# Stage 1's weight sums moved into the last first layer of stage 0, and the f64 conversion paced 11 and 17 steps a stage

## The chip, the cores and the metric

The kernel runs on one core of one Trainium2 chip. The metric is the time of one execution on the device in microseconds. The core has five instruction streams that work in parallel and wait for one another by semaphores: PE (matrix products), DVE (vector), ACT (activations and copies), POOL (elementwise), and SP, which here only issues DMAs. Each executes its own stream in order, so an instruction that waits holds all that stand behind it on its engine.

## The reference, cut to what matters

```
attention: scores = q k^T / 8, a window of 64 positions back, softmax, times v
x = attn_out as (1152 tokens, 512)
moe:   p = probs / sum(probs);  out = sum over e of p[:, e] * (relu(x @ w1[e]) @ w2[e])
       w1: (4, 512, 1024)   w2: (4, 1024, 512)
moe2:  h = out @ w_in;  g = max(h, 0) + alpha * min(h, 0);  result = g @ w_out
       w_in: (512, 2048)    w_out: (2048, 512)
```

All of it is wanted in float32. The weights of the last part come as float64 and are read as pairs of 32-bit words.

## The kernel before

**Stages.** The hidden dimension is cut into stages of 512 columns: stages 0 to 7 for the four experts, 8 to 11 for the last part. A stage has a first layer (x times w1) and a second layer (h times w2, added up in `acc`). Every float32 operand is split into a rounded high part and a low part (names ending in h and l); a product is three matmuls of the parts. The high part is made by ACT (`split`, L219), the low part by DVE (`low`, L212).

**Stage 0** runs with the attention, in four chunks of tokens: `LC(c)` is the first layer of chunk c (4 units), `BC(c)` its second layer (2 or 3 units). The last chunk, `LC(3)` and `BC(3)`, comes after the attention.

**Stages 1 to 11** make the first layer by seven half-size products of sums and differences of blocks in place of eight (units `A(s,p,i)`, i from 0 to 6, p=0 for tokens 0 to 511 and p=1 for 512 to 1151, each for two halves u of the columns). For that, sums of the weight blocks (`w_sums`, L187, tile `sr`, four instructions for each u) and of the token blocks (`x_sum`, L384, tile `tr`) are needed, and both are split: weights into `wf` by `w_split`, in the parts A11, A22 and SA1 (SA1 is the four sums), tokens into `xt`. The results of the products are combined in `product`: s, z and u are copies of the first, second and third product by ACT (L433) before the next product adds onto the same PSUM bank; later DVE adds the fourth, fifth and sixth to them (`total`, L437). So PE's third product (bank X again) waits for ACT's copy s, the fifth for ACT's copy u, and the seventh, in bank X once more, waits until DVE's total z has read the bank. The second layer has units `B(s,p,t)`, four for p=0, five for p=1, 12 matmuls each; DVE adds each to `acc` (L559).

**The order of the work** is written out by hand: `order` lists the units, `plan(unit, fn, ...)` hangs side work behind a unit, and every engine's stream is the order in which this Python code issues. From the last first layer on, the low part of a split is issued one unit after its high part (`late["wait"]`, `settle`). A weight load (`load_w`, tile `ws`, two buffers) is issued behind the last unit that uses the tile two loads earlier.

**The conversion.** The f64 weights of stages 8 to 11 are turned into float32 in 32 blocks during stages 1 to 7 (`conv_steps`) and stored in DRAM (`cv`). One block takes three steps, called a, b and c here:

- a: DVE L289 and POOL L290, L291 finish the block before; then ACT L277 and L278 begin this one from its loaded words (`wd`, two buffers).
- b: DVE L280 and L281, and SP's store of a finished block.
- c: DVE L284, and SP's load of the block two further on.

`pace` says how many steps follow a unit: one after each of the first three product units of A(s,0) and of A(s,1) from stage 2 on, two after each of the nine B units of stage 1, one after each B unit of stages 2 to 6. So stage 1 has 18 steps and stages 2 to 6 have 15 each, stage 7 has 6.

**Order around stage 1.** The sums of stage 1's weights hang on unit X1, between LC(3) and BC(3), on DVE for u=0 and on POOL for u=1. The token sums and splits for p=1 hang on the four units of LC(3) and the first three of A(1,0), all sums on POOL.

Of the kernel before, what the change touches and what calls it, by code (L numbers as in the profile page):

```python
# [26 lines left out]
def tile_kernel(ctx, tc, q, k, v, probs, w1, w2, w_in, w_out, alpha, out):  # L27
    nc = tc.nc
# [26 lines left out]
    NCH = len(CHUNK) - 1  # L55
# [33 lines left out]
    xr = [xr0, xr1[:, 0:KD * LEN[1]].rearrange("p (k t) -> p k t", k=KD)]  # L89
# [5 lines left out]
    for c in range(1, NCH):  # L95
        n = CHUNK[c + 1] - CHUNK[c]
# [68 lines left out]
    A11, A12, A22, SA1, SA2, SA3, SA4 = range(7)  # L165

    def w_block(s, u, i, j):
        t = ws_t[1, s]
        if s >= S1:
            return t[:, 2 * u + i, 2 * j * P:2 * (j + 1) * P].rearrange("p (k m) -> p k m", k=2)  # L170
        c = (2 * u + i) * P
        return t[:, 2 * j:2 * j + 2, c:c + P]

    def w_sums(s, u, e):
        if (s == 1 or s >= S1) and u == 1:
            t4 = late["mid"].tile([P, 1024], F32, tag="wd", bufs=2, name=f"sr{s}_{u}").rearrange(
                "p (o k m) -> p o k m", o=4, k=2)
# [389 lines left out]
    def raw2(p):  # L567
        return late[f"raw{p}"]
# [7 lines left out]
    with tc.manual_schedule():  # L576
# [104 lines left out]
        def plan(unit, fn, tid, *args):  # L681
            work.setdefault(at[unit], []).append((fn, tid, args))
# [2 lines left out]
            plan(("LC", 0, f), split_w2, (2, 0), 0, f)  # L685
        for s in range(1, NST):
            if s == 1:
                for u, e in enumerate((nc.vector, nc.gpsimd)):
                    plan(("X1",), w_sums, (1, s), s, u, e)
                b = [("BC", NCH - 1, t) for t in range(2)]  # L690
                for u, part, unit in ((0, A11, ("X1",)), (0, A22, ("X1",)), (0, SA1, b[0]), (1, A11, b[0]), (1, A22, b[0]), (1, SA1, b[1])):
                    plan(unit, w_split, (1, s), s, u, part)
            else:
                b = [("B", s - 1, x, t) for x in range(2) for t in range(NTT[x])]
                if s == S1 + 1:
                    b = [("B", S1, 1, t) for t in (3, 3, 4, 4, 0, 1)]
# [23 lines left out]
        for unit, p, splits, sums, (o, w) in changes:  # L720
# [5 lines left out]
            for f in sums:  # L726
                e = nc.vector if unit[0] == "B" and p else nc.gpsimd
                plan(unit, lambda *a: x_sum(a[0], raw2(a[0]), *a[1:]), (0, S1) if p == 0 else None, p, f, o, w, e)
        lc = [("LC", NCH - 1, f) for f in range(NF)] + [("A", 1, 0, i) for i in range(3)]
        for n, splits, sums in ((0, (0,), (1,)), (1, (0, 1), (2,)), (2, (2,), (3,)), (3, (), (4,)),  # L730
                                (4, (3,), ()), (5, (5,), ()), (6, (4,), ())):
            for o, w in half[1]:
                for f in splits:
                    if f == 0 and o == w * n:
                        plan(lc[n], x_first, None, 1, xr[1], o, w)
                    elif f:
                        plan(lc[n], x_split, None, 1, xr[1], f % 5, o, w)
# [25 lines left out]
        def pace(op, s=0, p=0, i=0):  # L763
            if op not in "AB" or s >= S1 or (s, op) in ((1, "A"), (S1 - 1, "B")):
                return 0
            return int(i < 3) if op == "A" else 1 + (s == 1)

        late["steps"] = conv_steps()
        pend = []
        for i, unit in enumerate(order):  # L770
            op = unit[0]
# [35 lines left out]
            for _ in range(pace(*unit)):  # L807
                next(late["steps"], None)
# [48 lines left out]
```

## Time and profile before

| what | value |
| --- | --- |
| median of 3 runs | 647.77 us (647.1 to 648.51) |
| the profiled execution | 647.18 us |
| its span, first to last instruction | 645.4 us |
| mean granted PE clock | 0.992 |
| busy: PE, DVE, ACT, POOL | 616.2, 469.8, 310.1, 288.9 us |

The profile is of one execution. Busy time counts instructions in flight; matmuls overlap, so the time that a run of them takes is read from the starts. The granted clock is a share of PE's full speed. In the timeline "[4.32 <-ACT s L433]" behind a row means that the engine had been idle 4.32 us and that the instruction it then waited for was ACT's on line 433. Where several matmuls stand in one row, xcount tells how many.

### The profile page before, as it was taken

The page shows a single profiled execution, that of the slowest core. Times are in us where ns is not written, and L with a number is a line of the kernel's source. Part 1 is how long each engine was busy: PE and PEld are TensorE (multiplying, and loading weights), DVE is VectorE, ACT ScalarE, POOL GpSimd, SP SyncE. Part 2 cuts the span into 40 slices and gives each one's busy share as a digit, 9 for nine tenths or more (in the row PEclk, how much of TensorE's full clock was granted, in tenths as well). Part 3 has the DMA queues.
Part 4 walks back from the last instruction along what each step waited for, and adds up shares of the span by engine and source line. Part 5 has one row for each costly group of instructions (what it writes and reads, how often), then busy time and mean ns, then how long its engine had stood idle before and what let it go on. Part 6 is the DMA issues. An engine that isn't in the chain of part 4 may idle for free.

```text
span 645.4 us, 10914 instructions
## 1 busy us (share of the span) xinstructions
PE 616.2 (95%) x4032; PEld 549.8 (85%) x4032; DVE 469.8 (73%) x937; ACT 310.1 (48%) x783; POOL 288.9 (45%) x303
## 2 busy tenths in 40 slices
PE   4799998997899999999999999999999999999998
PEld 3678887986898988988988988988897998988986
DVE  4765648879889889889889888866685474574652
ACT  5545534542561651641742642634766670760730
POOL 4645663235455345335435435524744290390440
PEclk9899999999899999999999999999999999999999
DMA  9841002215533433434334234001301011010012
GB/s 327 287 149 60 16 2 100 97 49 177 166 114 102 161 125 116 136 132 135 121 120 160 102 115 163 34 1 66 132 0 66 2 67 65 1 66 1 2 49 99
DMA packets 31654, 62.61 MB, mean 97 GB/s; under 512 B 2288, under 2 KB 11760, under 8 KB 30576
## 3 DMA queue, kind: packets, MB, share of 16 engines
q1 hardware_dynamic: 31600, 61.90, 27.6%
q8 instruction: 32, 0.52, 0.3%
q14 instruction: 22, 0.18, 0.1%
HBM read 51.14 MB, written 10.75 MB: 96 GB/s over the span
## 4 chain that ended last, share of the span: by engine, by line
PE 73%; DVE 16%; ACT 4%; DMA 3%; issue 2%; POOL 1%; SPq 0%; DVEq 0%; ACTq 0%; POOLq 0%
PE o L540 39%; PE X L426 17%; PE Z L426 7%; PE W L426 4%; DVE w2l L212 3%; DMA ws<-in_moe_w_dram 2%; PE oc L528 2%; PE h L495 2%; DVE ct L280 2%; DVE wfl L212 2%; DVE ct L284 2%; DVE ct L281 2%; ACT p L321 1%; ACT w2h L219 1%; POOL hl L521 1%
## 5 line engine op out<-in xcount | busy, mean ns | idle before, releaser
L540 PE MATMUL o<-w2h,hl 128*128 128x512 f32 (+1 forms) x400 | 155.7, 389 | 0.6 <-POOL hl L521 0.5
L540 PE MATMUL o<-w2l,hh 128*128 128x512 f32 (+1 forms) x400 | 155.6, 389 | 0.4 <-ACT hh L520 0.4
L540 PE MATMUL o<-w2h,hh 128*128 128x512 f32 (+1 forms) x400 | 154.9, 387 | 0.0
L290 POOL TENSOR_TENSOR ct<-ct 128x512 f32<-128x512 f32 x32 | 41.5, 1296 | 147.4 <-DVE ct L289 66.0
L540 PEld LDWEIGHTS o<-w2h,hl 128*128 128x128 f32 x400 | 75.1, 188 | 18.4 <-POOL hl L521 3.2
L540 PEld LDWEIGHTS o<-w2l,hh 128*128 128x128 f32 x400 | 75.1, 188 | 15.1 <-ACT hh L520 0.6
L540 PEld LDWEIGHTS o<-w2h,hh 128*128 128x128 f32 x400 | 75.2, 188 | 14.7
L559 DVE SCALAR_TENSOR_TENSOR acc<-o,pn,acc 128x512 f32<-128x512 f32 x63 | 47.1, 748 | 31.8 <-PE o L540 31.5
L426 PE MATMUL X<-xth,wfl 128*128 128x256 f32 (+1 forms) x264 | 58.7, 304 | 6.9 <-ACT s L433 4.3
L212 DVE SCALAR_TENSOR_TENSOR w2l<-ws,w2h 128x512 fp32r<-128x512 f32 x48 | 41.8, 878 | 29.3 <-ACT w2h L219 29.1
L426 PE MATMUL X<-xth,wfh 128*128 128x256 f32 (+1 forms) x264 | 57.1, 298 | 0.0
L426 PE MATMUL X<-xtl,wfh 128*128 128x256 f32 (+1 forms) x264 | 57.0, 298 | 0.0
L187 POOL TENSOR_TENSOR sr<-ws 128x256 f32<-128x256 f32 x42 | 42.3, 1007 | 27.4 <-DVE wfl L212 17.8
L521 POOL TENSOR_TENSOR hl<-s,hh 128x256 fp32r<-128x256 f32 (+1 forms) x16 | 13.9, 887 | 88.0 <-ACT hh L520 88.0
L426 PEld LDWEIGHTS X<-xth,wfl 128*128 128x128 f32 x264 | 42.7, 191 | 9.6 <-ACT s L433 4.5
L433 ACT ACTIVATE s<-X 128x256 f32<-128x256 f32 (+1 forms) x44 | 17.8, 410 | 64.0 <-PE X L426 64.0
L291 POOL TENSOR_TENSOR ct<-ct 128x512 f32<-128x512 f32 x32 | 47.0, 1469 | 2.5
L278 ACT ACTIVATE ct<-wd 128x512 f32<-128x512 f32 x32 | 21.4, 668 | 55.2 <-DVE ct L284 55.2
L563 DVE TENSOR_TENSOR acc<-o,acc 128x512 f32<-128x512 f32 (+1 forms) x28 | 18.8, 671 | 38.2 <-PE o L540 38.2
L426 PEld LDWEIGHTS X<-xth,wfh 128*128 128x128 f32 x264 | 43.1, 192 | 0.0
L426 PEld LDWEIGHTS X<-xtl,wfh 128*128 128x128 f32 x264 | 43.1, 192 | 0.0
L321 ACT ACTIVATE p<-sm,st 128x128 f32<-128x128 f32 x72 | 28.0, 390 | 27.7 <-DVE st L318 27.7
(161 smaller groups left out, 1444.7 us busy)
## 6 DMA issues: line engine op xcount, KB each, us to landing
ws<-in_moe_w_dram SPq DMA_DIRECT2D x16, 1024.0 KB, 6.0
wd<-in_moe_w_in_dram SPq DMA_DIRECT2D x16, 512.0 KB, 3.7
cv<-ct SPq DMA_DIRECT2D x32, 256.0 KB, 2.4
wd<-in_moe_w_out_dram SPq DMA_DIRECT2D x16, 512.0 KB, 3.6
ws<-cv SPq DMA_DIRECT2D x8, 1024.0 KB, 4.8
v<-in_v_dram SPq DMA_DIRECT2D x16, 256.0 KB, 5.7
q<-in_q_dram SPq DMA_DIRECT2D x6, 384.0 KB, 6.5
out_dram<-acc SPq DMA_DIRECT2D x8, 256.0 KB, 2.0
```

Source lines behind the costliest of these rows:

```text
L187: e.tensor_tensor(out=t4[:, o], in0=x, in1=y, op=op)
L212: nc.vector.scalar_tensor_tensor(out=lv, in0=src, scalar=1.0, in1=hv.bitcast(F32), op0=ALU.mult, op1=ALU.subtract)
L278: nc.scalar.activation(out=a, in_=top.bitcast(F32), func=AF.Abs, scale=LIFT)
L290: nc.gpsimd.tensor_tensor(out=y, in0=y, in1=e, op=ALU.mult)
L291: nc.gpsimd.tensor_tensor(out=y, in0=r, in1=y, op=ALU.add)
L321: nc.scalar.activation(out=pt[:, hp, :], in_=sm[:, hp, :], func=AF.Exp, scale=-1.0, bias=st[:, 0, hp:hp + 1], accum_out=st[:, 1, hp:hp + 1])
L426: nc.tensor.matmul(ps, lhsT=w[:, d, :], rhs=x[:, d, :], start=(first and m == 0), stop=(m == 5), skip_group_check=True)
L433: nc.scalar.activation(out=t, in_=ps, func=AF.Copy)
L521: nc.gpsimd.tensor_tensor(out=hl, in0=g, in1=hh.bitcast(F32), op=ALU.subtract)
L540: nc.tensor.matmul(ps, lhsT=h_t[s, p, f][a][:, t * P:(t + 1) * P], rhs=w_t[2, s, f][b][:, cols], start=(n == 0), stop=(n == 3 * NF - 1))
L559: nc.vector.scalar_tensor_tensor(out=at, in0=ps, scalar=sc, in1=at, op0=ALU.mult, op1=ALU.add)
L563: nc.vector.tensor_tensor(out=at, in0=ps, in1=at, op=ALU.add)
```

## The change

Three edits. The sums of stage 1's weights are made on POOL for both u, behind the first two units of LC(3), in the tile that otherwise holds loaded f64 words (`wd`), for u=0 as well. The token sums and splits for p=1 are spread anew: sums 1, 2 and 3 on DVE behind LC(3,2), LC(3,3) and BC(3,0), sum 4 on POOL behind BC(3,2); the weight splits behind X1 and BC(3) are put in another order, A22 last. `pace` gives every B unit one step, and one more in p=1 after the units with odd t: 9 + 2 = 11 steps in a second layer, in stage 1 as in stages 2 to 6. With the six in the products that is 11 steps in stage 1 and 17 in stages 2 to 6.

```
-        if (s == 1 or s >= S1) and u == 1:
+        if s == 1 or s >= S1 and u == 1:
...
-                for u, e in enumerate((nc.vector, nc.gpsimd)):
-                    plan(("X1",), w_sums, (1, s), s, u, e)
-                b = [("BC", NCH - 1, t) for t in range(2)]
-                for u, part, unit in ((0, A11, ("X1",)), (0, A22, ("X1",)), (0, SA1, b[0]), (1, A11, b[0]), (1, A22, b[0]), (1, SA1, b[1])):
+                lc, b = [[(k, NCH - 1, t) for t in range(3)] for k in ("LC", "BC")]
+                for u in range(2):
+                    plan(lc[u], w_sums, (1, s), s, u, nc.gpsimd)
+                for u, part, unit in ((0, A11, ("X1",)), (1, A11, b[0]), (0, SA1, b[0]), (1, SA1, b[1]),
+                                      (0, A22, b[2]), (1, A22, b[2])):
...
-        for n, splits, sums in ((0, (0,), (1,)), (1, (0, 1), (2,)), (2, (2,), (3,)), (3, (), (4,)),
-                                (4, (3,), ()), (5, (5,), ()), (6, (4,), ())):
+        for unit, splits, sums, e in ((lc[0], (0, 5), (), None), (lc[1], (0,), (), None), (lc[2], (), (1,), nc.vector),
+                                      (lc[3], (1,), (2,), nc.vector), (bc[0], (), (3,), nc.vector), (bc[1], (2,), (), None),
+                                      (bc[2], (3,), (4,), nc.gpsimd), (("A", 1, 0, 1), (4,), (), None)):
...
-            return int(i < 3) if op == "A" else 1 + (s == 1)
+            return int(i < 3) if op == "A" else 1 + (p == 1 and i % 2)
```

**DVE, from the last first layer to the second layer's second unit.** `hcl` is the low part of stage 0's hidden values, `xtl` a token split, `tr` a token sum, `sr` the weight sums, `wfl` a weight split, `acc` the eviction of a second-layer unit `oc`. Before:

```order
L507 SCALAR_TENSOR_TENSOR hcl_3_1399<-h_3_3_1385,hch_3_1398 128x384
L212 SCALAR_TENSOR_TENSOR xtl_1311<-tr_2_0_1355,xth_1310 128x2x160
L212 SCALAR_TENSOR_TENSOR xtl_1311<-tr_2_160_1357,xth_1310 128x2x160
L187 TENSOR_TENSOR sr_0_1412<-ws_1_462 128x256
L187 TENSOR_TENSOR sr_0_1412<-sr_0_1412,ws_1_462 128x256
L187 TENSOR_TENSOR sr_0_1412<-ws_1_462 128x256
L187 TENSOR_TENSOR sr_0_1412<-ws_1_462,sr_0_1412 128x256
L534 TENSOR_SCALAR acc_80<-oc_0_1426,pn 128x512
L212 SCALAR_TENSOR_TENSOR wfl_0_1423<-ws_1_462,wfh_0_1422 128x512
L212 SCALAR_TENSOR_TENSOR wfl_0_1423<-ws_1_462,wfh_0_1422 128x256
L534 TENSOR_SCALAR acc_80<-oc_1_1447,pn 128x512
L212 SCALAR_TENSOR_TENSOR wfl_0_1423<-sr_0_1412,wfh_0_1422 128x1024
```

and after the change:

```order
L507 SCALAR_TENSOR_TENSOR hcl_3_1399<-h_3_3_1385,hch_3_1398 128x384
L384 TENSOR_TENSOR tr_2_0_1404<-xr_86,tr_1_0_1381 128x320
L384 TENSOR_TENSOR tr_2_160_1406<-xr_86,tr_1_160_1383 128x320
L212 SCALAR_TENSOR_TENSOR xtl_1311<-tr_1_0_1381,xth_1310 128x2x160
L212 SCALAR_TENSOR_TENSOR xtl_1311<-tr_1_160_1383,xth_1310 128x2x160
L534 TENSOR_SCALAR acc_80<-oc_0_1417,pn 128x512
L212 SCALAR_TENSOR_TENSOR wfl_0_1415<-ws_1_462,wfh_0_1414 128x512
L384 TENSOR_TENSOR tr_3_0_1436<-xr_86 128x320
L384 TENSOR_TENSOR tr_3_160_1438<-xr_86 128x320
L534 TENSOR_SCALAR acc_80<-oc_1_1440,pn 128x512
L212 SCALAR_TENSOR_TENSOR wfl_1_1433<-ws_1_462,wfh_1_1432 128x512
L212 SCALAR_TENSOR_TENSOR wfl_0_1415<-sr_0_1329,wfh_0_1414 128x1024
```

The four weight sums are gone from DVE and six token sums have come in; the split of u=1's loaded weight (`wfl_1` from `ws`, 512) now stands before the splits of the sums.

**ACT, start of stage 2's first layer.** `s`, `z`, `u` are the copies of products, `wd` the loaded f64 words, `w2h` a split of the second layer's weight. Before:

```order
L277 ACTIVATE ct<-wd_1929 128x512
L278 ACTIVATE ct<-wd_1929 128x512
L433 ACTIVATE s_0_0_2004<-X_0_0_1997 128x256
L433 ACTIVATE s_0_1_2013<-X_0_1_2006 128x256
L277 ACTIVATE ct<-wd_1970 128x512
L278 ACTIVATE ct<-wd_1970 128x512
L433 ACTIVATE z_0_0_2027<-Z_0_0_2020 128x256
L433 ACTIVATE z_0_1_2036<-Z_0_1_2029 128x256
L219 ACTIVATE w2h_0_2038<-ws_2_1704 128x512
L433 ACTIVATE u_0_0_2050<-X_0_0_1997 128x256
```

and after:

```order
L277 ACTIVATE ct<-wd_1907 128x512
L278 ACTIVATE ct<-wd_1907 128x512
L433 ACTIVATE s_0_0_1979<-X_0_0_1972 128x256
L433 ACTIVATE s_0_1_1988<-X_0_1_1981 128x256
L433 ACTIVATE z_0_0_2000<-Z_0_0_1993 128x256
L433 ACTIVATE z_0_1_2009<-Z_0_1_2002 128x256
L219 ACTIVATE w2h_0_2011<-ws_2_1704 128x512
L277 ACTIVATE ct<-wd_1948 128x512
L278 ACTIVATE ct<-wd_1948 128x512
L433 ACTIVATE u_0_0_2025<-X_0_0_1972 128x256
```

The L277 and L278 that stood between `s` and `z` now stand behind `z` and `w2h_0` and in front of `u`; and what they read is the fifth block of the conversion where it was the seventh.

**DVE, from the last unit of stage 2's second layer to the total s of stage 3.** `ct` is the conversion's tile (L280, L281: step b; L284: step c; L289: step a), `w2l` the low split of the second layer's weight. Before:

```order
L559 SCALAR_TENSOR_TENSOR acc_80<-o_1_4_2471,pn,acc_80 128x512
L284 SCALAR_TENSOR_TENSOR ct<-wd_2373,ct 128x512
L289 TENSOR_SCALAR ct<-ct 128x512
L280 TENSOR_SCALAR ct<-ct 128x512
L281 TENSOR_SCALAR ct<-ct 128x512
L212 SCALAR_TENSOR_TENSOR w2l_0_2530<-ws_3_2224,w2h_0_2529 128x512
L284 SCALAR_TENSOR_TENSOR ct<-wd_2431,ct 128x512
L437 TENSOR_TENSOR s_0_0_2495<-W_0_0_2558,s_0_0_2495 128x256
L437 TENSOR_TENSOR s_0_1_2504<-W_0_1_2569,s_0_1_2504 128x256
L484 SCALAR_TENSOR_TENSOR hl_0_0_2567<-s_0_0_2495,hh_0_0_2566 128x256
L212 SCALAR_TENSOR_TENSOR w2l_1_2553<-ws_3_2224,w2h_1_2552 128x512
```

and after:

```order
L559 SCALAR_TENSOR_TENSOR acc_80<-o_1_4_2452,pn,acc_80 128x512
L289 TENSOR_SCALAR ct<-ct 128x512
L280 TENSOR_SCALAR ct<-ct 128x512
L281 TENSOR_SCALAR ct<-ct 128x512
L284 SCALAR_TENSOR_TENSOR ct<-wd_2409,ct 128x512
L212 SCALAR_TENSOR_TENSOR w2l_0_2511<-ws_3_2199,w2h_0_2510 128x512
L289 TENSOR_SCALAR ct<-ct 128x512
L437 TENSOR_TENSOR s_0_0_2478<-W_0_0_2541,s_0_0_2478 128x256
L437 TENSOR_TENSOR s_0_1_2487<-W_0_1_2552,s_0_1_2487 128x256
L484 SCALAR_TENSOR_TENSOR hl_0_0_2550<-s_0_0_2478,hh_0_0_2549 128x256
L212 SCALAR_TENSOR_TENSOR w2l_1_2534<-ws_3_2199,w2h_1_2533 128x512
L437 TENSOR_TENSOR z_0_0_2499<-X_0_0_2471,z_0_0_2499 128x256
```

In stage 3 the order of the steps behind the first three products was a, b, c (L289; L280, L281; L284) and is b, c, a, so that L289, which releases POOL's L290 and L291, is the last DVE instruction before the total `s`.

## Rows read from the trace of the kernel before

**Rows 1.** The page, busy us by engine, share of the span, instructions.
```profile
PE 616.2 (95%) x4032; PEld 549.8 (85%) x4032; DVE 469.8 (73%) x937; ACT 310.1 (48%) x783; POOL 288.9 (45%) x303
```

**Rows 2.** Timeline of PE, stage 8: start, us, engine, line, op, out<-in, shapes.
```profile
501.31 0.40 PE L426 MATMUL X<-xah,wfl 128*128 128x256 f32 x2
...
511.37 0.46 PE L426 MATMUL X<-xah,wfl 128*128 128x320 f32 x2
...
523.70 0.40 PE L540 MATMUL o<-w2l,hh 128*128 128x512 f32 x1
```

**Rows 3.** Timeline of PE, stages 1 and 2; brackets: idle before, and its releaser.
```profile
103.97 0.48 PE L426 MATMUL X<-xah,wfl 128*128 128x256 f32 x2
...
106.68 0.50 PE L426 MATMUL X<-xah,wfl 128*128 128x256 f32 x2 [1.75 <-DVE wfl L212]
...
117.90 0.46 PE L426 MATMUL X<-xah,wfl 128*128 128x320 f32 x2
...
130.23 0.40 PE L540 MATMUL o<-w2l,hh 128*128 128x512 f32 x1
...
154.73 0.40 PE L426 MATMUL X<-xah,wfl 128*128 128x256 f32 x2
...
162.08 0.79 PE L426 MATMUL X<-xth,wfl 128*128 128x256 f32 x2 [4.32 <-ACT s L433]
...
173.79 0.46 PE L426 MATMUL X<-xah,wfl 128*128 128x320 f32 x2
...
186.44 0.40 PE L540 MATMUL o<-w2l,hh 128*128 128x512 f32 x1
...
210.95 0.40 PE L426 MATMUL X<-xah,wfl 128*128 128x256 f32 x2
```

**Rows 4.** Timeline of PE, stage 3 and the start of stage 7.
```profile
221.15 0.46 PE L426 MATMUL X<-xah,wfl 128*128 128x320 f32 x2
...
233.82 0.40 PE L540 MATMUL o<-w2l,hh 128*128 128x512 f32 x1
...
400.45 0.40 PE L426 MATMUL X<-xah,wfl 128*128 128x256 f32 x2
```

**Rows 5.** Windows: length, busy us of PE, PEld, DVE, ACT, POOL, PEclk, DMA share, GB/s.
```profile
187.00:211.00 24.00, 24.00 (x108) 19.85 (x107) 20.39 (x29) 8.29 (x15) 11.91 (x10) 1.00 0.33 116
...
162.00:167.00 5.00, 4.92 (x23) 4.92 (x24) 3.65 (x5) 1.78 (x6) 3.18 (x3) 0.50 0.79 226
```

**Rows 6.** Timeline of DVE before stage 1.
```profile
98.90 1.09 DVE L187 TENSOR_TENSOR sr<-ws 128x256 f32<-128x256 f32 x1
...
105.95 1.01 DVE L212 SCALAR_TENSOR_TENSOR wfl<-ws,wfh 128x512 fp32r<-128x512 f32 x2
```

**Rows 7.** The page, groups by line: count, busy us, mean ns, idle before.
```profile
L187 POOL TENSOR_TENSOR sr<-ws 128x256 f32<-128x256 f32 x42 | 42.3, 1007 | 27.4 <-DVE wfl L212 17.8
...
L290 POOL TENSOR_TENSOR ct<-ct 128x512 f32<-128x512 f32 x32 | 41.5, 1296 | 147.4 <-DVE ct L289 66.0
...
L291 POOL TENSOR_TENSOR ct<-ct 128x512 f32<-128x512 f32 x32 | 47.0, 1469 | 2.5
```

**Rows 8.** Timelines of SP's queue and of ACT, start of stage 2.
```profile
156.39 0.33 SPq L155 DMA_DIRECT2D wd<-in_moe_w_out_dram  x1
...
160.53 0.66 ACT L277 ACTIVATE ct<-wd 128x512 f32<-128x512 uint32 x1 [3.49 <-DMA wd<-in_moe_w_out_dram]
```

**Rows 9.** Timelines of DVE and of POOL, stages 2 and 3.
```profile
194.54 0.43 DVE L281 TENSOR_SCALAR ct<-ct 128x512 uint32<-128x512 uint32 x1
...
214.54 1.36 POOL L291 TENSOR_TENSOR ct<-ct 128x512 f32<-128x512 f32 x1
...
214.78 1.40 DVE L281 TENSOR_SCALAR ct<-ct 128x512 uint32<-128x512 uint32 x1
...
217.31 0.74 DVE L437 TENSOR_TENSOR s<-W,s 128x256 f32<-128x256 f32 x2
...
219.15 0.42 DVE L437 TENSOR_TENSOR z<-X,z 128x256 f32<-128x256 f32 x1
```

More of the change, by code (lines that the diff above doesn't have):

```diff
@@ L728, in tile_kernel @@
                 plan(unit, lambda *a: x_sum(a[0], raw2(a[0]), *a[1:]), (0, S1) if p == 0 else None, p, f, o, w, e)
-        lc = [("LC", NCH - 1, f) for f in range(NF)] + [("A", 1, 0, i) for i in range(3)]
-        for n, splits, sums in ((0, (0,), (1,)), (1, (0, 1), (2,)), (2, (2,), (3,)), (3, (), (4,)),
-                                (4, (3,), ()), (5, (5,), ()), (6, (4,), ())):
+        lc, bc = [[(k, NCH - 1, t) for t in range(4)] for k in ("LC", "BC")]
+        for unit, splits, sums, e in ((lc[0], (0, 5), (), None), (lc[1], (0,), (), None), (lc[2], (), (1,), nc.vector),
+                                      (lc[3], (1,), (2,), nc.vector), (bc[0], (), (3,), nc.vector), (bc[1], (2,), (), None),
+                                      (bc[2], (3,), (4,), nc.gpsimd), (("A", 1, 0, 1), (4,), (), None)):
             for o, w in half[1]:
                 for f in splits:
-                    if f == 0 and o == w * n:
-                        plan(lc[n], x_first, None, 1, xr[1], o, w)
+                    if f == 0 and o == w * unit[2]:
+                        plan(unit, x_first, None, 1, xr[1], o, w)
                     elif f:
-                        plan(lc[n], x_split, None, 1, xr[1], f % 5, o, w)
+                        plan(unit, x_split, None, 1, xr[1], f % 5, o, w)
             for f in sums:
                 for o, w in half[1]:
-                    plan(lc[n], x_sum, None, 1, xr[1], f, o, w, nc.gpsimd)
+                    plan(unit, x_sum, None, 1, xr[1], f, o, w, e)
         plan(("A", 1, 0, 5), big_as, None, "ct")
```

## Prediction

> **What bounds the kernel now.** I read the page's busy shares first: PE is busy 616.2 of 645.4 us [rows 1], so what can be won is what PE waits for or does slowly. The timeline of PE comes next: one row for the start of each half of a stage gives what a stage costs, and rows with an idle time in brackets say for whom PE waited. Stage 8 waits for nothing: its first layer takes 10.06 us for tokens p=0 (501.31 to 511.37) and 12.33 for p=1 (to 523.70), 22.39 together [rows 2]. Against that:
>
> - Stage 1: p=0 takes 13.93 (103.97 to 117.90), 3.87 too many, 1.75 of it one wait for the DVE weight split wfl; p=1 takes 12.33, none too many [rows 3].
> - Stage 2: p=0 takes 19.06 (154.73 to 173.79), 9.00 too many, 4.32 of it one wait for ACT's eviction s; p=1 takes 12.65, 0.32 too many [rows 3].
> - Stage 3: p=0 takes 10.20 (210.95 to 221.15), 0.14 too many; p=1 12.67 (to 233.82), 0.34 too many. Stages 3 to 6 are alike: from 210.95 to 400.45 are 189.50 us, 4 x 47.38, and a stage without waits is 22.39 + 24.50 (a second layer, 130.23 to 154.73) = 46.89. So four times 0.48 [rows 3, 4].
>
> Together 3.87 + 9.32 + 1.92 = 15.1 us. That is about all that this change can win, since it touches little before 85 us or after stage 7. The 9.00 is more than its waits: after the wait of 4.32 the granted clock is 0.50 from 162 to 167 us (the 1.2 GHz level), and a row of two matmuls that takes 0.40 elsewhere takes 0.79 [rows 3, 5].
>
> **Part 1, the order around stage 1.** Before, DVE reaches the four sums for u=0 only at 98.90, because POOL made the token sums first and DVE their splits; and the split that PE waits for, wfl of u=1, begins at 105.95 although its source is the loaded weight [rows 6]. After, all eight sums stand on POOL, which comes to them near 86, some 20 us before PE asks for their splits: eight times the 1.01 of the page's row is 8.1, so they end near 94 [rows 7]. DVE gets six of the token sums (128x320, about 0.45 each: the total z of 128x256 takes 0.42 [rows 9]), 2.7 us, in place of four weight sums of about 0.9. Walking DVE from the end of the last first layer, each eviction where PE frees it, I get wfl of the weights ready near 100.5 (u=0) and 102.6 (u=1), and the two splits of the sums near 103.8 and 105.9. PE asks for these at 103.97, 104.69, 105.41 and 106.13 (steps of 10.06/14). All four are in time, the last by 0.2. The token splits of p=1 end near 109.5, before the totals, so z is no longer late. I take 0.1 left of 3.87. Bounds: 0, or 1.2 if DVE is one split late. What hides POOL's sums is the last first layer and the second layer behind it; if POOL came to them more than 8 us later, PE would wait.
>
> **Part 2, fewer steps in stage 1.** The wait of 4.32 in stage 2 is ACT's queue: L277 started at 160.53, when the load issued at 156.39 had landed (4.1 us), and the evictions s stand behind it [rows 8]. Before, 18 steps run in stage 1's second layer and three more in stage 2's first products, so a load is asked for about every 4 us and ACT stands on the newest. After, 11 steps run there. The load that ACT needs next in stage 2 is asked for when DVE does L284 in the fourth of the five p=1 units, some 1.2 us before stage 2 starts at T, and with the same 4.1 it lands at T + 2.9. ACT comes to its L277 at about T + 4.0, behind s, z and the first w2h, so it waits for nothing; the eviction u behind it is due at T + 5.75 and done at T + 5.5. So the 9.00 goes, but what is late next has to be found.
>
> **Part 3, 17 steps in place of 15.** 15 is five blocks of three steps, so every stage has met its first products with the same three, a, b, c. 17 shifts them: stages 2 and 5 get c, a, b, stages 3 and 6 get b, c, a, and stage 4 alone a, b, c as before. Step a starts POOL's pair (L290, L291). A DVE instruction that works in SBUF alone loses what is left of a running POOL instruction: L281 takes 0.43 at 194.54 with POOL idle, and 1.40 at 214.78 beside L291, which began at 214.54 [rows 9]. The Trainium skill's page SBUF — State Buffer, section "Who interferes with whom", says the same and more: whichever of the two engines issues second is blocked until the first is done, POOL as well as DVE. The trace agrees for DVE; for POOL this row shows nothing of it, L291 took 1.36 with L281 held beside it. What full blocking would make of the time is the second rival.
>
> What matters is the chain on DVE that ends at z: PE's seventh product needs z at T + 8.62 (6/7 of 10.06). In stage 3 now, with T = 210.95, s starts at 217.31 (T + 6.36) and z ends at 219.57 (T + 8.62): no slack at all [rows 3, 9].
>
> - Order b, c, a: the POOL pair now starts when s does. The walk is eviction, L289, L280, L281 (held by the L290 of the last step a), L284 (held by its L291), w2l, L289: s starts near T + 6.0, POOL's pair runs from T + 6.1 to 8.9 (1.30 + 1.47 [rows 7]). Between s and z stand hl and w2l, both with two SBUF inputs, and each loses one POOL instruction: w2l starts at T + 8.9 and takes about 0.7, z 0.42, end at T + 10.0. That is 1.4 late. In p=1 POOL's pair falls behind the totals, and 0.34 goes to 0.
> - Order c, a, b: eviction, L280, L281, L284, L289 end near T + 4.0; POOL's pair runs to T + 6.9; L280 and L281 are held by one of it each and end near T + 7.4; from s to the end of z are 2.26: T + 9.7, 1.1 late. In p=1 the same walk gives about the present 0.34.
> - Order a, b, c: 0.48 as now.
>
> No row shows either new order, so bounds: 0 at the least (POOL's pair misses the chain), and the whole pair, 2.77, at the most. I take the walks, 1.1 and 1.4, which lie between.
>
> **The sum.** Left over after: stage 1 0.1; stage 2 1.1 + 0.34; stage 3 1.4; stage 4 0.48; stage 5 1.1 + 0.34; stage 6 1.4. That is 6.3 of 15.1, a gain of 8.8. The two more steps in a second layer (at most 2 us of DVE by L280, L281 and L284 with POOL idle) lie in its idle time: DVE is busy 20.4 of 24.0 us from 187 to 211 [rows 5]; without that cover they would lengthen the chain to z by as much. The profiled execution took 647.18 us, 1.8 more than its span and 0.6 under the median of the runs, 647.77. 647.18 - 8.8 = 638.4.
>
> **The rivals.**
>
> 1. The new orders cost nothing: POOL's pair and DVE's chain slip past each other. For it: a DVE instruction that starts just before POOL's is not held. Against it: the chain has no slack now. Left over are 0.1 + 0.34 + 0.48 + 0.34, say 1.5 with the 0.14 of p=0: 647.2 - 13.6 = 633.6.
> 2. The whole POOL pair falls into the chain in four stages: 4 x 2.77 + 1.3 = 12.4 left, 647.2 - 2.7 = 644.5. For it: DVE's instruction lost the full remainder in the row. Against it: part of the pair lies where DVE waits for the W product anyway.
> 3. Slower: ACT still stands on the load, now in front of u. The place is L277 in stages 2 and 5 (order c, a, b). If the load takes over 6 us from its issue rather than 4.1, u is late; with a wait as long as now, PE's clock falls as it did at 162. At the price of stage 2 now, 9.0 twice in place of 1.1 twice, 22.1 is left over: 647.2 + 7.0 = 654.2. It decides from the point where each of the two costs over 5.5 us. For it: 1 MB weight loads go to the same queue. Against it: they are asked for some 5 us earlier.
> 4. The change doesn't do what it says: stage 1's weights come no earlier, since the sums' tiles lie in space that the attention part must free first, and stage 2 still meets its load. Then the 15.1 stay: 647.
>
> **How the numbers follow.** Forecast 0.53, first rival 0.24, second 0.14, third 0.05, fourth 0.04. Within 0.2% (1.3 us, about what a measurement here can tell from no change) is the fourth; faster are the forecast and the first two, 0.91; slower the third. The range from 633.0 to 643.5 holds the forecast, the first rival and the way to the second.
>
> **What would show it.** Right: after 84 us no wait of PE for wfl or s over 1 us; granted clock 1.00 from 104 to 260; the sums L187 of stage 1 all on POOL and ended before 95; stage 4's first layer as now; in stages 3 and 6 PE waits over 1 us for z before the seventh product of p=0, with L290 and L291 beside hl and w2l. Wrong: a PE wait for u in stages 2 or 5 (third rival), first layers of 22.4 in stages 2, 3, 5, 6 (first rival), or PE's first products of stage 1 still waiting for wfl.

## Result and the profile after

| what | before | after |
| --- | --- | --- |
| median, us | 647.5 (647.1 to 648.51, 4 runs) | 652.51 (652.07 to 652.87, 4 runs) |
| ratio of the times, 95% interval | | 1.0075 [1.0057, 1.0092] |
| span of the profiled execution | 645.4 | 650.8 |

The change makes the kernel 0.75% slower. The forecast was 638.4, with 633.0 to 643.5 as the range. Two executions of the kernels below, one of pair_bc (1220.56 us) and one of early_p0 (2125.35 us), were disturbed and stand in no median and no ratio.

The page's busy times after, answering to [rows 1]: PE works no more than before, so the time is in waits and in slow matmuls.

```profile
PE 617.6 (95%) x4032; PEld 552.2 (85%) x4032; DVE 469.9 (72%) x939; ACT 312.4 (48%) x783; POOL 284.1 (44%) x301
```

PE's timeline of the changed kernel, read as in [rows 2 to 4]: the first product of a half, and the rows with a long wait in brackets.

```profile
104.91 0.40 PE L426 MATMUL X<-xah,wfl 128*128 128x256 f32 x2
...
115.06 0.46 PE L426 MATMUL X<-xah,wfl 128*128 128x320 f32 x2
...
151.90 0.40 PE L426 MATMUL X<-xah,wfl 128*128 128x256 f32 x2
...
158.71 0.50 PE L426 MATMUL X<-xth,wfl 128*128 128x256 f32 x2 [0.91 <-ACT u L433]
...
163.16 0.50 PE L426 MATMUL X<-xth,wfl 128*128 128x256 f32 x2 [1.32 <-DVE z L437]
...
201.58 0.40 PE L426 MATMUL X<-xah,wfl 128*128 128x256 f32 x2
...
213.44 0.80 PE L426 MATMUL X<-xth,wfl 128*128 128x256 f32 x2 [2.95 <-DVE z L437]
...
254.53 0.40 PE L426 MATMUL X<-xah,wfl 128*128 128x256 f32 x2
...
262.98 0.51 PE L426 MATMUL X<-xth,wfl 128*128 128x256 f32 x2 [2.55 <-ACT u L433]
...
405.84 0.40 PE L426 MATMUL X<-xah,wfl 128*128 128x256 f32 x2
```

What each stage's first layer takes over the 10.06 + 12.33 us without waits, worked out from such rows (the second layers add 0.03 at most each, 0.1 in the sum; the forecast had no term for stage 7):

| stage | 1 | 2 | 3 | 4 | 5 | 6 | 7 | sum |
| --- | --- | --- | --- | --- | --- | --- | --- | --- |
| before | 3.9 | 9.3 | 0.5 | 0.5 | 0.5 | 0.5 | 0.2 | 15.3 |
| forecast | 0.1 | 1.4 | 1.4 | 0.5 | 1.4 | 1.4 | | 6.3 |
| after | 0.1 | 2.8 | 6.0 | 4.5 | 2.8 | 3.3 | 0.2 | 19.7 |

Stage 1 came out as worked out, and two thirds of stage 2's 9 us went. But stages 3 to 6, which had lost nearly nothing, lose 14.8 us more. (The rest of the 5.4 us between the spans is stage 0: stage 1 starts 0.9 later, 104.91 against 103.97. That start lies between 103.7 and 105.0 in the kernels below, whatever their steps are.)

The waits of PE that have grown, from the list of waits (us in total, times, longest); before, those for z were 1.6 us in all and those for u 0.7:

```profile
PE X L426 <- DVE z L437: 7.8, 4, 3.0
...
PE X L426 <- ACT u L433: 4.3, 3, 2.5
```

Part of the loss follows the waits. After the wait of 2.95 the row of two matmuls takes 0.80, as in [rows 3, 5], and in the windows (us, busy time of each engine, granted clock) the granted clock from 212.7 to 219.5 us is 0.50, the 1.2 GHz level:

```profile
212.70:219.50 6.80, 6.06 (x25) 6.06 (x26) 5.49 (x14) 2.65 (x7) 2.69 (x3) 0.50 0.08 30
```

It is 0.50 once more from 263.9 to 267.3, behind the wait of 2.55. PE's waits in stages 1 to 7 add up to 12.6 of the 19.7 us; in the two stretches at half the clock it is busy for 9.5 us, which costs some 5 more (an estimate: half of that time).

**Why z and u are late.** DVE at the end of stage 1's second layer, after the change; stage 2 starts at T = 151.90:

```profile
147.63 0.43 DVE L289 TENSOR_SCALAR ct<-ct 128x512 uint32<-128x512 uint32 x1
147.97 0.74 DVE L559 SCALAR_TENSOR_TENSOR acc<-o,pn,acc 128x512 f32<-128x512 f32 x1
148.63 1.14 DVE L280 TENSOR_SCALAR ct<-ct 128x512 f32<-128x512 f32 x1
149.81 1.40 DVE L281 TENSOR_SCALAR ct<-ct 128x512 uint32<-128x512 uint32 x1
151.12 0.74 DVE L559 SCALAR_TENSOR_TENSOR acc<-o,pn,acc 128x512 f32<-128x512 f32 x1
151.78 0.68 DVE L284 SCALAR_TENSOR_TENSOR ct<-wd,ct 128x512 uint32<-128x512 uint32 x1
...
152.91 0.74 DVE L559 SCALAR_TENSOR_TENSOR acc<-o,pn,acc 128x512 f32<-128x512 f32 x1
```

and POOL beside it:

```profile
148.20 1.29 POOL L290 TENSOR_TENSOR ct<-ct 128x512 f32<-128x512 f32 x1 [3.82 <-DVE ct L289]
149.57 1.35 POOL L291 TENSOR_TENSOR ct<-ct 128x512 f32<-128x512 f32 x1
```

L289 starts POOL's pair, and L280 and L281 come right behind: L280 takes 1.14 beside L290, L281 1.40 beside L291 (0.43 with POOL idle, [rows 9]). DVE has no idle time here. Its last eviction of the layer is at 152.91, when PE is 1.0 us into the next stage (behind stages 2 to 6 it is 1.0 to 2.4 here, and 0.2 in the kernel before), so L284 runs at 151.78 and the load behind it is late too. SP and ACT in stage 2, then in stage 3 (T = 201.58), answering to [rows 8]:

```profile
152.52 0.34 SPq L155 DMA_DIRECT2D wd<-in_moe_w_out_dram  x1
```

```profile
157.15 0.68 ACT L277 ACTIVATE ct<-wd 128x512 f32<-128x512 uint32 x1 [1.22 <-DMA wd<-in_moe_w_out_dram]
...
158.29 0.64 ACT L433 ACTIVATE u<-X 128x256 f32<-128x256 f32 x2
```

```profile
199.01 0.92 SPq L144 DMA_DIRECT2D ws<-in_moe_w_dram  x1
...
203.52 0.37 SPq L155 DMA_DIRECT2D wd<-in_moe_w_in_dram  x1
```

```profile
209.92 0.66 ACT L277 ACTIVATE ct<-wd 128x512 f32<-128x512 uint32 x1 [2.75 <-DMA wd<-in_moe_w_in_dram]
...
211.04 0.71 ACT L476 ACTIVATE hh<-s 128x256 fp32r<-128x256 f32 x2
```

The load is asked for at T + 0.6 in stage 2 and T + 1.9 in stage 3, and from its issue to ACT's L277 pass 4.6 and 6.4 us (in stage 3 a weight load was issued 4.5 us ahead of it on the same queue). ACT stands on it, and u in stage 2, hh and with it z in stage 3, come behind. In stage 3 DVE is late by itself too: its total s starts at 208.78, T + 7.2, where it started at T + 6.4 before.

### The profile page after: what moved, and what is told of

The parts are those of the page before. It is cut to its first block, busy times and chain, and to the rows that moved or that the text cites. A ratio compares the mean times of both kernels' runs of the same rounds, so it can differ in the third digit from the quotient of the medians.

```text
span 650.8 us, 10925 instructions
## 1 busy us (share of the span) xinstructions
PE 617.6 (95%) x4032; PEld 552.2 (85%) x4032; DVE 469.9 (72%) x939; ACT 312.4 (48%) x783; POOL 284.1 (44%) x301
## 4 chain that ended last, share of the span: by engine, by line
PE 73%; DVE 13%; DMA 6%; ACT 3%; POOL 2%; issue 2%; SPq 0%; DVEq 0%; ACTq 0%; POOLq 0%
PE o L540 32%; PE X L426 18%; PE Z L426 9%; PE W L426 4%; PE h L495 3%; PE oc L528 3%; DMA wd<-in_moe_w_out_dram 2%; DVE ct L280 2%; DVE wfl L212 2%; DVE ct L281 2%; DMA wd<-in_moe_w_in_dram 2%; DVE acc L559 2%; DMA ws<-in_moe_w_dram 2%; DVE ct L284 1%; PE pv L352 1%
## 5 line engine op out<-in xcount | busy, mean ns | idle before, releaser
L290 POOL TENSOR_TENSOR ct<-ct 128x512 f32<-128x512 f32 x32 | 42.7, 1333 | 109.5 <-DVE ct L289 70.0
L540 PEld LDWEIGHTS o<-w2h,hh 128*128 128x128 f32 x400 | 75.2, 188 | 14.8
L426 PE MATMUL X<-xth,wfl 128*128 128x256 f32 (+1 forms) x264 | 58.7, 304 | 12.6 <-DVE z L437 7.8
L187 POOL TENSOR_TENSOR sr<-ws 128x256 f32<-128x256 f32 x44 | 40.7, 925 | 57.8 <-DVE wfl L212 51.9
L426 PEld LDWEIGHTS X<-xth,wfl 128*128 128x128 f32 x264 | 42.8, 192 | 14.8 <-DVE z L437 8.8
L291 POOL TENSOR_TENSOR ct<-ct 128x512 f32<-128x512 f32 x32 | 47.1, 1472 | 2.5
L278 ACT ACTIVATE ct<-wd 128x512 f32<-128x512 f32 x32 | 21.4, 667 | 40.7 <-DVE ct L284 40.7
```

Of the source, the lines that this page charges most:

```text
L278: nc.scalar.activation(out=a, in_=top.bitcast(F32), func=AF.Abs, scale=LIFT)
L290: nc.gpsimd.tensor_tensor(out=y, in0=y, in1=e, op=ALU.mult)
L291: nc.gpsimd.tensor_tensor(out=y, in0=r, in1=y, op=ALU.add)
L426: nc.tensor.matmul(ps, lhsT=w[:, d, :], rhs=x[:, d, :], start=(first and m == 0), stop=(m == 5), skip_group_check=True)
L540: nc.tensor.matmul(ps, lhsT=h_t[s, p, f][a][:, t * P:(t + 1) * P], rhs=w_t[2, s, f][b][:, cols], start=(n == 0), stop=(n == 3 * NF - 1))
```

## Experiments

Two theories at the start. **Density**: two more steps in a second layer bring the steps so close together that DVE falls behind, and load, s, u and z with it. **Shift**: the forecast's Part 3, the order in which a stage's first products meet a, b and c, only larger than worked out. "Left over" is the sum of the table above, of the profiled execution alone, which can lie off the median: 1.8 us above it in load_early (650.89), 1.8 below it in after_room (644.39). Each ratio is to the kernel before on the same chip.

| kernel | us | ratio, 95% | left over |
| --- | --- | --- | --- |
| order_only | 644.22 | 0.9932 [0.9914, 0.9951] | 11.9 |
| pace_only | 654.65 | 1.009 [1.0057, 1.0122] | 21.9 |
| even_abc | 643.16 | 0.992 [0.9905, 0.9935] | 10.5 |
| even_bca | 644.39 | 0.9939 [0.9921, 0.9956] | 12.1 |
| dense_abc | 653.78 | 1.0081 [1.0054, 1.0108] | 22.1 |
| load_early | 649.13 | 1.0012 [0.9997, 1.0028] | 17.9 |
| pool_small | 634.55 | 0.9789 [0.9765, 0.9812] | 1.8 |
| start_early | 636.75 | 0.9819 [0.9797, 0.9841] | 4.8 |
| pair_bc | 653.32 | 1.0081 [1.0066, 1.0096] | 21.2 |
| early_pair | 641.63 | 0.9915 [0.9899, 0.9931] | 9.6 |
| extra_p0 | 646.47 | 0.9974 [0.9963, 0.9985] | 14.3 |
| early_p0 | 641.44 | 0.989 [0.9874, 0.9906] | 10.3 (early_p0_look) |
| after_room | 646.18 | 0.9987 [0.9965, 1.0008] | 11.9 |

### The two parts of the change: order_only, pace_only

order_only is the changed kernel with the old pace, pace_only the kernel before with the new one.

```
order_only:  return int(i < 3) if op == "A" else 1 + (s == 1)
pace_only:   return int(i < 3) if op == "A" else 1 + (p == 1 and i % 2)
```

> The new order around stage 1 alone, with the pace of before (18 steps in stage 1, 15 in stages 2 to 6). Three theories of why the changed kernel is slower. Density: the order is good, and the second step behind some units of the second layers is what costs, because L280 and L281 then meet POOL's pair of the step before, DVE falls behind, asks for the next load late, and ACT's L277 stands on that load with PE's evictions behind it. Shift: the order is good, and what costs is the order c, a, b or b, c, a of the steps behind a stage's first products. Order: the new order itself costs something later. Density and shift: stage 1's first layer loses its 3.8 us of waits and stage 2 keeps its 9.0, 647.5 - 3.8 = 643.7. Order: 647 or more.

> The new pace alone (11 and 17 steps), with the order of before around stage 1. Density and shift: the changed kernel's losses in stages 2 to 6 and the 3.8 us of stage 1 back, 652.5 + 3.8 = 656.3. Order: below 652.

Both as expected. The new order alone gains 0.7% (stage 1 loses 0.1, stage 2 still loses 9.7, stages 3 to 6 stay at 0.5); the new pace alone loses 0.9%. The loss of the change is the pace.

### Density or shift: even_abc, even_bca, dense_abc

In the changed kernel: one step per second-layer unit (the steps left over go into stage 7's products); the same with stage 1 given one more, so that every stage meets b, c, a; and 18 steps in stages 2 to 5 (stage 6 has the 13 that are left) with a, b, c in every stage.

```
even_abc:   return int(i < 3 or s == S1 - 1) if op == "A" else 1
even_bca:   return int(i < 3 or s == S1 - 1) if op == "A" else 1 + ((s, p, i) == (1, 0, 3))
dense_abc:  return int(i < 3) if op == "A" else 1 + (p == 1 and i % 2 == 1) + (s > 1 and p == 1 and i == 2) + ((s, p, i) == (1, 0, 3))
```

> The changed kernel with one step behind every unit of the second layers and none with two: 9 steps in stage 1, 15 in stages 2 to 6, 14 in stage 7 (one behind each product unit), so that every stage meets its first products with a, b, c. Density: stages 2 to 6 lose 0.5 us each instead of 2.8 to 6.0, stage 7 with its eight more steps 1 to 2; of the 19.6 us that the changed kernel loses in stages 1 to 7 some 4 are left: 637. Shift: the same 637. Order: 643 or more.

> As the kernel with one step behind every unit, but with one step more in stage 1 (10), behind a p=0 unit, so that all of stages 2 to 6 meet their first products with b, c, a. Density: within 1.5 us of the kernel with a, b, c, about 637. Shift: 1.4 us more in each of five stages, 7 more than that kernel, 644.

> The changed kernel with 12 steps in stage 1 and 18 in stages 2 to 6 (a third second step behind a p=1 unit), so that every stage meets its first products with a, b, c as in the kernel before, but the steps stand as close as in the changed kernel or closer. Density: stages 2 to 5 lose 3 us or more each, 650 or more. Shift: 0.5 each, 635.

Shift falls as the main cause: with the old order a, b, c in every stage and 18 steps, 22.1 us are left over, against 19.7 with the shifted orders and 17 steps. With 15 steps a stage loses 0.5 in order a, b, c and 1.1 in order b, c, a. Both sparse kernels missed the 637, since the many steps in stage 7's products cost 7.9 (even_abc) and 6.3 (even_bca) there; even_bca's 644.39 is next to the 644 of Shift for this reason alone, and it lies 1.2 above even_abc (3.2 more in stages 2 to 6, 1.7 less in stage 7), where Shift had 7.

### The load or POOL's pair: load_early, pool_small

load_early asks for the load a step earlier (behind step b); pool_small makes POOL's two instructions on 8 columns.

```
load_early:
-   ... in0=top, scalar=SIGN, in1=au, ...        # L284, and load_d(n + 2) behind it
+   ... in0=au, scalar=SIGN, in1=au, ...         # load_d(n + 2) now behind store() in step b
pool_small:
-   nc.gpsimd.tensor_tensor(out=y, in0=y, in1=e, op=ALU.mult)
+   nc.gpsimd.tensor_tensor(out=y8, in0=y8, in1=e8, op=ALU.mult)     # and the add likewise
```

> The changed kernel with L284 reading only ct, not the loaded words, and SP's load of the block two further on issued behind step b instead of step c; the sign of the converted weights is left out, the instructions and their sizes stay. If what PE meets is the load asked for late, so that ACT's L277 stands in front of PE's evictions: the waits for u and s go and those for z shrink to what the sparse order showed (1.1 in stages 3 and 6, as much in 2 and 5, 0.5 in 4), of 19.7 us some 6 are left, 639. If DVE's own chain beside POOL's pair is what counts and not the load: 649 to 652.

> The changed kernel with POOL's pair of the conversion (L290, L291) on 8 of 512 columns; the rest of each converted block lacks its low words' part and the exponent correction. If POOL's pair, by holding L280 and L281, is what makes DVE late and so the load: nearly all of the 19.7 us goes, 3 left, 636. If the steps are too close for the load whatever POOL does: waits for the load stay, 645 or more.

The earlier load takes 3.4 us off the median, which leaves it in the second of its two expectations. In the profiled execution stages 3 and 4 lose 2.4 and 2.5 less (in stage 4 the wait for u is gone), but stages 2 and 6 lose 1.6 and 1.5 more: there the granted clock is 0.50, from 163.6 to 167.0 and from 365.0 to 368.4, behind waits for z of 2.07 and 2.12. PE still waits 9.8 for z in all. Without POOL's pair nearly all is gone, 1.8 left over, with steps, loads and orders of the changed kernel. DVE there, around the same place (stage 2 starts at 151.68):

```profile
151.88 0.75 DVE L560 SCALAR_TENSOR_TENSOR acc<-o,pn,acc 128x512 f32<-128x512 f32 x1 [0.85 <-PE o L541]
152.55 0.42 DVE L280 TENSOR_SCALAR ct<-ct 128x512 f32<-128x512 f32 x1
```

The eviction now waits for PE and not PE's results for DVE. The groups of DVE's instructions by line (count | busy us, mean ns | idle before) say what a block costs. After the change:

```profile
L281 DVE TENSOR_SCALAR ct<-ct 128x512 uint32<-128x512 uint32 x32 | 30.2, 945 | 1.1
L280 DVE TENSOR_SCALAR ct<-ct 128x512 f32<-128x512 f32 x32 | 29.4, 919 | 4.2 <-ACT ct L278 4.2
L284 DVE SCALAR_TENSOR_TENSOR ct<-wd,ct 128x512 uint32<-128x512 uint32 x32 | 29.3, 917 | 0.6
L289 DVE TENSOR_SCALAR ct<-ct 128x512 uint32<-128x512 uint32 x32 | 14.5, 453 | 0.8
```

and in pool_small:

```profile
L284 DVE SCALAR_TENSOR_TENSOR ct<-wd,ct 128x512 uint32<-128x512 uint32 x32 | 23.0, 719 | 0.6
L281 DVE TENSOR_SCALAR ct<-ct 128x512 uint32<-128x512 uint32 x32 | 16.6, 518 | 1.1
L280 DVE TENSOR_SCALAR ct<-ct 128x512 f32<-128x512 f32 x32 | 16.0, 501 | 2.9 <-ACT ct L278 2.9
L289 DVE TENSOR_SCALAR ct<-ct 128x512 uint32<-128x512 uint32 x32 | 14.5, 454 | 0.8
```

3.2 us a block against 2.2 (sums of the means). The hold itself is not new: in the kernel before the four means are 928, 876, 793 and 504 ns, 3.1 us a block. So pool_small shows that the loss needs the hold, not that the change made it larger. It also makes the load earlier, since L284 is no longer late, and frees the splits of the first layer from POOL's pair, so it does not part these causes; load_early moves the load with DVE's steps as they were.

### Fewer steps a stage: start_early

One step per second-layer unit, and the conversion begins three steps earlier, in stage 1's p=1 products; `pace` gives stage 7 eight steps.

```
-   if op not in "AB" or s >= S1 or (s, op) in ((1, "A"), (S1 - 1, "B")):
+   if op not in "AB" or s >= S1 or (s, op) == (S1 - 1, "B") or (s, op, p) == (1, "A", 0):
-   return int(i < 3) if op == "A" else 1 + (p == 1 and i % 2)
+   return int(i < 3 or s == S1 - 1 and i == 6) if op == "A" else 1
```

> One step behind every second-layer unit as in the even a, b, c kernel (10.5 us lost, 7.9 of them in stage 7, which had 14 steps), but the conversion begins in stage 1's first layer: three steps behind the first products of p=1, so stage 1 has 12, stages 2 to 6 have 15, and stage 7 eight, two more behind its last product. Density: stage 7 loses under 1, stage 1's p=1 under 1, stages 2 to 6 0.5 each: 643.2 - 7 = 636. Shift the same. If the load is late in stage 1 or the DVE chain there has no room, up to 3 us more, 639.

As expected, and 1.8% faster than the kernel before: stages 2 to 6 lose 0.5 each, stage 7 2.3.

### Is it that b follows a at once? pair_bc, early_pair

Both put the extra steps so that b and c share a unit and a stands alone: pair_bc everywhere, early_pair in stages 2 and 3 of start_early, with six steps in stage 7.

```
pair_bc:     return int(i < 3) if op == "A" else 1 + (p == 1 and i % 2 == 0)
early_pair:  return int(i < 3) if op == "A" else 1 + (s in (2, 3) and p == 1 and i % 2 == 0)
```

> The changed kernel with the extra step after even t of p=1 in place of odd t, so the second layer reads bc, a, bc, a, bc there: 12 steps in stage 1 and 18 in stages 2 to 6, every stage's products meet a, b, c. It has as many steps and the same order at the products as dense_abc (653.8), and differs in one thing: a step b never follows its step a in the same unit. If the cause is L280 and L281 beside the POOL pair that the step a just ahead of them started, DVE loses 1 us a block (L281 alone) in place of 2.1, keeps up with PE, and stages 2 to 6 fall to about 0.5 each: 2.8 us left over in all, about 635, and not above 639. If the number of steps in a second layer is the cause (DVE's or the queue's total work), it stays with dense_abc, 651 to 655.

> start_early with six steps in stage 7 in place of eight, and in stages 2 and 3 the extra step after even t of p=1 (18 steps there, 15 in stages 4 to 6, 12 in stage 1). If pairing b with c costs nothing, stages 2 and 3 stay at 0.5 each and stage 7's 2.15 goes to 0.2: 2 us under start_early's 636.75, about 635. If the number of steps decides, stages 2 and 3 cost about 4 each, as in the changed kernel: 642.

Pairing b with c gains nothing, and the second expectation of each holds: pair_bc is as slow as dense_abc, and in early_pair exactly the two stages behind the denser second layers, 3 and 4, lose 3.9 each. DVE in pair_bc, at the end of stage 2's second layer (stage 3 starts at 201.99), shows what becomes of the unit between a and b:

```profile
197.78 0.42 DVE L289 TENSOR_SCALAR ct<-ct 128x512 uint32<-128x512 uint32 x1
198.11 0.74 DVE L559 SCALAR_TENSOR_TENSOR acc<-o,pn,acc 128x512 f32<-128x512 f32 x1
198.77 1.14 DVE L280 TENSOR_SCALAR ct<-ct 128x512 f32<-128x512 f32 x1
199.94 1.40 DVE L281 TENSOR_SCALAR ct<-ct 128x512 uint32<-128x512 uint32 x1
201.43 0.69 DVE L284 SCALAR_TENSOR_TENSOR ct<-wd,ct 128x512 uint32<-128x512 uint32 x1
```

DVE is already behind, so the unit's eviction does not wait for PE and L280 stands 1.0 us behind L289, inside POOL's pair. The distance in the program is worth nothing here, since the engine is late.

### Where is there room? extra_p0, early_p0, after_room

The windows of p=1's half of a second layer, with DVE's busy time as the third engine's: before (stage 2), then after (stage 2).

```profile
197.30:210.95 13.65, 13.65 (x61) 11.27 (x61) 12.55 (x16) 2.97 (x4) 8.86 (x8) 1.00 0.41 136
```

```profile
187.94:201.58 13.64, 13.64 (x62) 11.27 (x60) 13.27 (x18) 3.52 (x5) 9.91 (x9) 1.00 0.35 116
```

Before, DVE had 1.1 us of idle time in this half, where both extra steps went; after, 0.4. extra_p0 moves them to p=0's units, early_p0 does the same to early_pair; after_room leaves them and shortens DVE's evictions.

```
extra_p0:    return int(i < 3) if op == "A" else 1 + (p == 0 and i % 2)
early_p0:    return int(i < 3) if op == "A" else 1 + ((s in (2, 3) and p == 0) * (0, 1, 0, 2, 0)[i])
after_room:
-   ...(out=at, in0=ps, scalar=sc, in1=at, ...)
+   h = DM // 2 if s else DM
+   ...(out=at[:, 0:h], in0=ps[:, 0:h], scalar=sc, in1=at[:, 0:h], ...)
```

> The changed kernel with its two extra steps of a second layer after the odd units of p=0 in place of those of p=1: the same 11 and 17 steps and the same shifted orders at the products, nothing else. DVE is busy 12.49 of 13.65 us in p=1's half of a second layer with one step a unit, and 8.42 of 10.87 in p=0's (start_early, stage 3): 1.2 us of room against 2.4. If the extra steps hurt because p=1's half has no room for their 2 us, they fit in p=0's, and what is left is what the shifted orders cost, 1.1 a stage in stages 2, 3, 5 and 6 and 0.5 in stage 4, with 0.1 in stage 1: 6 us left over, 638, within 636 to 641. If the number of steps in a second layer decides, wherever they stand, 650 to 653 as in the changed kernel.

> early_pair (641.6) with its three extra steps of stages 2 and 3 after units 1 (one) and 3 (two) of p=0 in place of p=1: 18 steps there, a, b, c at all products, six steps in stage 7. If room in p=1's half decides, the 3.6 that stages 3 and 4 each lost there fall to 1 or less and stage 7 stays without a wait: 7 us under early_pair at best, 634.5 to 637. If the number of steps decides, 641.6 as in early_pair.

> The changed kernel, with DVE's eviction L559 of stages 1 to 7 on the first 256 of a unit's 512 columns (the other half of the second layer's sum is left out): 0.42 us in place of 0.75, nine times a second layer, 3.0 us of DVE; all steps, loads, POOL's pair and the orders stand as they are. If DVE's room in a second layer decides, the two extra steps (two thirds of a block of 3.2 us, 2.1) fit again, and what is left over is what the shifted orders cost, 6 us in all: 636 to 640. If the number of blocks decides by the loads or by ACT's and POOL's queues, DVE's room does nothing: 649 to 653.

> The kernel of early_p0, for its profile. If DVE's room over the whole second layer decides, stages 3 and 4, which follow the two second layers of 12 steps, lose 2.5 to 4 each, as in early_pair, with DVE without idle time for the last 10 us of the second layer before; stages 2, 5, 6 and 7 lose 0.5 or less. If something else made up its 641.8 (the later stages), stages 3 and 4 lose under 1.

extra_p0 is between its two expectations: 6 us better than the changed kernel, 8 short of 638. In its stage 2 DVE still has 2.1 us of idle time in p=0's half, where it had 2.5 in the kernel before, and 0.1 in p=1's, where it had 1.1: the two steps have taken 0.4 from the half in which they stand and 1.0 from the other. early_p0 gained nothing on early_pair that is clear of the spread. early_p0_look, the same kernel (643.16, one run), shows stages 3 and 4 losing 3.7 and 4.9 and the others 0.5 or less. So p=0's half has little usable room: with three more steps there DVE once waits for POOL, which has the weight sums and two pairs in a row, and the next load stands on SP behind the store of what that pair makes:

```profile
191.49 0.43 DVE L289 TENSOR_SCALAR ct<-ct 128x512 uint32<-128x512 uint32 x1 [1.19 <-POOL ct L290]
```

```profile
193.09 0.33 SPq L256 DMA_DIRECT2D cv<-ct  x1
193.58 0.38 SPq L155 DMA_DIRECT2D wd<-in_moe_w_in_dram  x1
```

after_room gives DVE 2.4 us a second layer back (nine evictions of 0.48 in place of 0.75; 0.42 was expected) and lies between its two expectations: 6.3 us under the changed kernel by the medians, 11.9 left over in place of 19.7 in the profiled execution. DVE's room is a part of the loss, not all. In stages 2 and 5 DVE's last eviction of the layer before starts 0.2 us into the stage, as in the kernel before, and both stages still lose 2.0; in stage 2 ACT's L277 starts 5.2 us after its load was issued. In its stage 3 (start 200.37, order b, c, a) DVE is on time up to s, at 206.69, and then ACT and POOL make z late (ACT's L277 reads a load issued 5.3 us before, at 201.59; the profile names no releaser for its wait):

```profile
206.91 0.68 ACT L277 ACTIVATE ct<-wd 128x512 f32<-128x512 uint32 x1 [1.07 <-issue]
...
208.07 0.71 ACT L476 ACTIVATE hh<-s 128x256 fp32r<-128x256 f32 x2
```

```profile
208.51 1.34 DVE L484 SCALAR_TENSOR_TENSOR hl<-s,hh 128x256 fp32r<-128x256 f32 x1 [1.07 <-ACT hh L476]
209.77 1.21 DVE L212 SCALAR_TENSOR_TENSOR w2l<-ws,w2h 128x512 fp32r<-128x512 f32 x1
```

```profile
208.29 1.27 POOL L291 TENSOR_TENSOR ct<-ct 128x512 f32<-128x512 f32 x1
209.52 0.90 POOL L187 TENSOR_TENSOR sr<-ws 128x256 f32<-128x256 f32 x1
```

hl takes 1.34 beside L291 of POOL's pair, and w2l 1.21 beside the weight sum behind it (L187), where they take 0.43 and 0.68 in stage 2. This is the kind of hold that Part 3's walk priced at 1.4, on top of ACT's wait; that POOL's weight sums hold w2l too was not in the walk.

## Why the prediction was wrong

- **Part 1 held.** 0.1 is left of 3.87. POOL makes the eight weight sums from 86.80 on, in steps of 0.7 to 0.8 rather than 1.01, to 92.66 (94 forecast), and the last split of them, wfl of u=1, begins at 105.77 and ends at 106.99, when PE asks for it at 107.05:

```profile
86.80 0.74 POOL L187 TENSOR_TENSOR sr<-ws 128x256 f32<-128x256 f32 x1
...
91.92 0.74 POOL L187 TENSOR_TENSOR sr<-ws,sr 128x256 f32<-128x256 f32 x1
```

```profile
105.77 1.22 DVE L212 SCALAR_TENSOR_TENSOR wfl<-sr,wfh 128x1024 fp32r<-128x1024 f32 x1
```

- **The step that failed** is the sentence of the sum "The two more steps in a second layer (at most 2 us of DVE by L280, L281 and L284 with POOL idle) lie in its idle time". Its cover, 20.4 of 24.0 us [rows 5], is a mean over both halves of the layer. The steps went into p=1's half, which had 1.1 us. And POOL was not idle: a block costs DVE 3.2 us (3.1 already in the kernel before), not 2.2. Two steps, two thirds of a block, are 2.1 us, so the price of 2 us was about right and the cover was what failed. The price that the sentence itself gave for lost cover, that they "would lengthen the chain to z by as much", 2 us in each of five stages, would have brought the sum to about 648; the measured 13.4 over the forecast's 6.3 is more, since a late DVE asks late for the load, and PE's clock falls behind the long waits (some 5 us by the estimate above). A late DVE also runs more of its steps inside POOL's pair, but that part is small: a block costs 3.06 us in start_early, 3.23 in the changed kernel and 3.40 in pair_bc. pace_only, dense_abc, pool_small and after_room show the first links; how the 13.4 divides among them is not settled, since load_early (3.4 less by the medians) and after_room (6.3 less) change both DVE's chain and the load's place in it (a block costs 3.34 in load_early), and no run has both edits.
- **Part 2 followed it, and had the load too short.** Of the 9.00 some 6.3 went, and the wait for s with them, but the load was to be asked for at T - 1.2 and land at T + 2.9. With DVE behind it was T + 0.6, and ACT had it 4.6 us later, not 4.1; in stage 3 it was 6.4, and 5.2 in after_room's stage 2. In stage 4 (order a, b, c, forecast unchanged at 0.5) the wait for u is 2.55.
- **Part 3 was near in size and beside the point.** Order b, c, a was to cost 1.4 in p=0 and nothing in p=1: even_bca measures 1.13 and 0.00 per stage, with one wait for z in each. The walk had both hl and w2l lose a POOL instruction; there w2l alone does (in stage 3 1.78 beside L291, hl 0.48). Order c, a, b was not tried alone.
- **The rivals.** The third had the sign and the mechanism, ACT on the load in front of u, but saw it in stages 2 and 5 alone and only from 5.5 us each; those two lost 2.8, and most of the loss is in stages 3, 4 and 6, where it named none. No rival had the density of the steps itself.
- **The signs.** Waits for z over 1 us in stages 3 and 6 were to show the forecast right, and they came (2.95 and 2.13); so did the waits for u in stages 2 and 5 that were to show it wrong (0.91 and 0.88), and stage 4, which was to stay as it was, lost 4.5 in place of 0.5.

## What to carry to other kernels

Idle time that is to hide work must be read for the very stretch in which the work will stand, and the work priced with the neighbours that it will have there, not with the best of its rows. On an in-order engine a small deficit can grow, since being late moves instructions into another engine's way and puts off the loads issued behind them; 3.6 us of idle time in 24 did not take 2.1 us of work. Side work that is too dense was here better begun earlier than packed: start_early, three steps sooner and one a unit, is 1.8% faster than the kernel before.

## What the runs showed of the hardware

POOL is held by DVE as well. In after_room an L291 takes 2.15 us, where it takes 1.35 at 199.09; a DVE split of the weight sums, which takes 1.22 elsewhere, was in flight from 192.81 to 194.22, and L291 ends 1.14 behind it:

```profile
193.21 2.15 POOL L291 TENSOR_TENSOR ct<-ct 128x512 f32<-128x512 f32 x1
```

It is no single case. In the changed kernel seven of the 32 L291 take 1.62 to 2.22 us; a DVE split was in flight at the start of each, and each ends 1.14 to 1.16 us behind that split. The other 25 take 1.27 to 1.37. The Trainium skill's page SBUF — State Buffer, section "Who interferes with whom", says that the lock works in both directions, for DVE instructions with two SBUF inputs or in one of its two-port modes; the prediction had seen it for DVE alone, and these rows agree with the page for POOL too.

Where L280 falls against the pair also matters: it takes 0.42 when it begins in the gap between L290 and L291 (start_early at 149.64, with L290 ending at 149.62 and L291 beginning at 149.70; L291 then takes 1.51 and ends 1.15 behind L280), and 1.14 when L290 has run for 0.4 us (after, 148.63).

Behind the same waits of PE the clock fell in one stage and not in the others. In pair_bc PE waits some 1.25 us for u and 1.85 or 1.86 for z in each of the stages 3 to 6; only behind those in stage 4 is the granted clock 0.50, the 1.2 GHz level (265.0 to 268.4), and that stage loses 5.1 where the other three lose 3.9. The ten executions of load_early spread from 647.88 to 651.34; that the clock is why is not shown.
